# The first attention batch loaded without accumulating transfers: q and k summed by VectorE, v by remainders in the product, and a scheduler that counts issues, bytes and latency of transfers

## The chip, the cores and the metric

The kernel runs on one core of one Trainium2 chip. The metric is the device time of one execution in microseconds, from launch to end; the kernel before was run three times.

## What is computed

Three stages follow one another: a two-part attention, a gated MLP with an RMS norm ahead of it, and a second MLP with a squared ReLU.

```python
# q, k, v: (4 batches, 8 heads, 576 positions, 64), fp32; factor = 4, Sd = 144
q_d = q.reshape(B, H, Sd, factor, D).mean(axis=3)      # the same for k_d, v_d
out_d = sm_attn(q_d, k_d, v_d)                         # softmax attention over 144 means
out_up = np.repeat(out_d, factor, axis=2)
mask = np.abs(pos[:, None] - pos[None, :]) < factor    # local attention, 7 keys a row
out_local = softmax(where(mask, q @ k.T / 8, -1e9)) @ v
x = (out_up + out_local)                               # -> 2304 tokens x 512
xn = x / rms(x) * rms_g
h = silu(xn @ w_gate) * (xn @ w_val) @ w_out           # 512 -> 1536 -> 512
g = s * relu(h @ w_in) ** 2 + b                        # 512 -> 2048
return g @ w_out2                                      # 2048 -> 512
```

The change touches the means over four positions, q_d, k_d and v_d, of the first batch alone.

## The kernel before

The 2304 tokens are worked on in 8 blocks of 288 columns (TB); a batch of attention fills two blocks. A batch has four units, each a pair of heads on 128 partitions: `unit(b, hp)` with hp from 0 to 3 (line 547). A unit makes the local scores of 9 windows (`local`, line 558), the scores of the means (`sd`, lines 587 to 592, from the tile `qd`), both softmaxes, transposes, the product of the means' weights with v (`pvd`, lines 626 to 631, from the tile `vd`), the local product with v (lines 632 to 639), and writes the sum to X (line 645). Then come the squares for the norm; `norm` (line 661) sums them on TensorE, raises them to a power on GpSimd (line 671), spreads them on TensorE and writes X as two f16 halves (lines 679 to 685). The first matmul of the gated MLP (`moe1_gv`, line 793) needs all four units of the batch, that norm for its 288 columns, and part 0 of the gate and value weights.

The sums over four positions come from transfers. `load_unit` (line 517) loads the first of four remainders of q and k with a plain transfer from SyncE's queue (`qkr`, 128x288 f32) and adds the other three with transfers that GpSimd issues with `accum_op=ADD`; the same holds for v (`vr`, 72x256 f32). Transfers into the same tile follow one another, since each adds to what the one before has left. Unit (0,0) alone has q and k summed by VectorE, from the tile `qkT` that the local scores need anyway (`DVE_Q`, line 57, and line 583).

The weights come as 64-bit numbers: `fetch` (line 698) loads a piece into one of eight, then six, then three staging places with SyncE, and ScalarE (two operations) and VectorE (one) decode it. A staging place is free for the next piece when it is decoded. 32 pieces are the gate and value weights (four parts of eight), the next 12 are w_out. `prep_gv` (line 740) then scales and splits them in two f16 halves.

All of this is recorded as a list of operations with their tiles, and `Plan.schedule` (line 310) sets one static order for each engine and for the queues of SyncE and GpSimd; the engines run that order and wait on semaphores. The order comes from a list scheduler with costs: a transfer of GpSimd counts 1.0 for the issue and 3.5 to landing, one of SyncE keeps its queue busy for its bytes (lines 195 to 203). `STEPS` (line 47) is a list of seeds; each disturbs the priorities by `shaken` (line 92). `emit` (line 335) writes the instructions, and where the plan has a gap on TensorE ahead of the first MLP matmul it puts in filler matmuls (line 1131), whose result nobody reads. Every recorded operation has line 352 in the profile.

Batch 1's units are spread among the MLP products of blocks 0 and 1, whose order is a fixed chain. Their v tiles are the four pieces of `VS` (line 447), which in the kernel before also hold batch 0's v.

Of the kernel before, what the change touches and what calls it, by code (L numbers as in the profile page):

```python
# [2 lines left out]

# [19 lines left out]
NP = H // 2  # L23
# [18 lines left out]
RING0 = 15744  # L42
E23 = float(2 ** 23)
SWITCH = 0.095
REACH = 230.0
EARLY = 0.0
STEPS = (
# [5 lines left out]
)  # L53
TOGETHER = 30.0
PE_SUM = ()
PE_SQ = (0,)
DVE_Q = ((0, 0),)
DVE_MASK = (2, 3)
JS = (range(5), range(5, 9))
SIZE = {F32: 4, I32: 4, F16: 2, BF16: 2, U16: 2}  # L60
# [24 lines left out]
def cols(ap):  # L85
    n = 1
    for d in list(ap.ap)[1:]:
        n *= d[1]
    return n


def shaken(key, at, seed):

    r = random.Random(seed)
    key = list(key)
    if r.random() < 0.5:
        mid, width, size, share = r.uniform(0, REACH), r.choice((3, 10, 30)), r.choice((0.5, 2, 8)), r.choice((0.1, 0.5, 1))
        for k, t in enumerate(at):
            if abs(t - mid) < width and r.random() < share:
                key[k] += r.gauss(0, size)  # L100
    else:
        a, n, size = r.randrange(1000), r.choice((2, 5, 15, 40, 100)), r.choice((1, 4, 15))
        by, every = r.gauss(0, size), r.choice((1, 1, 2, 4))
        for k in range(a, a + n * every, every):
            key[k] += by
    return key


class Op:
    __slots__ = ("alts", "fn", "pred", "chain", "early", "tag")  # L110


class Plan:
# [36 lines left out]
    def put(self, alts, fn, reads, writes, chain=False):  # L150
        op = Op()
        op.alts, op.fn, op.chain, op.early = alts, fn, chain, self.early
        op.pred = self.touch(len(self.ops), reads, writes)
        self.ops.append(op)

    def record(self, engs, name, args, kw):
        if self.AP is None:
            self.AP = type(args[0] if args else kw["out"])
        aps = {k: v for k, v in kw.items() if isinstance(v, self.AP)}
        pos = [a for a in args if isinstance(a, self.AP)]  # L160
        outs = [aps.pop(k) for k in ("out", "accum_out") if k in aps]
        if pos:
            outs.append(pos.pop(0))
        ins = pos + list(aps.values())
        reads = [x for a in ins if a.space is not None and "DRAM" not in str(a.space) for x in span(a)]
        writes = [x for a in outs if "DRAM" not in str(a.space) for x in span(a)]
        if engs[0] == "PE":
            t, full = self.pe_time(name, kw)
            single = self.group is None
            if single:  # L170
                self.group = [[], [], [], 0.0, []]
            g = self.group
            g[0].append((name, args, kw))
            g[1].extend(reads)
            g[2].extend(writes)
            if g[4] and g[4][-1] != full:
                t += SWITCH
            g[3] += t
            g[4].append(full)
            if single:  # L180
                self.close()
            return
        big = [a for a in ins if cols(a) > 8 and a.space != PSUM]
        n = max(cols(a) for a in outs + ins)
        scal = sum(cols(a) == 1 for a in ins)
        alts = []
        for e in engs:
            if e == "DVE":
                occ = 0.065 + 1.042e-3 * n + (0.06 if scal else 0)
                alts.append((e, occ, occ + 0.15, len(big) > 1 and n > 32))  # L190
            elif e == "ACT":
                psum = any(a.space == PSUM for a in ins)
                occ = 0.06 + (0.85e-3 if psum else 0.95e-3) * n + 0.1 * scal + (0.09 if "accum_out" in kw else 0)
                alts.append((e, occ, occ + 0.17, False))
            elif e == "POOL" and name == "dma_start":
                alts.append((e, 1.0, 3.5, False))
            elif e == "POOL":
                occ = (0.9 if kw.get("op") == ALU.pow else 0.2) if n < 32 else 0.08 + 2.1e-3 * n * (0.9 if n > 500 else 1)
                alts.append((e, occ, occ + 0.15, n >= 32))
            else:  # L200
                kb = cols(outs[0] if "DRAM" not in str(outs[0].space) else ins[0]) * 4 * 128 / 1e3
                occ = max(0.43, kb / 390)
                alts.append((e, occ, occ + 2.0, False))
        self.put(alts, [(name, args, kw)], reads, writes)

    def pe_time(self, name, kw):
        n = cols(kw["out"])
# [31 lines left out]
    def run(self, pred, succ, chain, key, back):  # L239
# [2 lines left out]
        left = [len(p) for p in pred]  # L242
        ready = [0.0] * n
        engs = ("PE", "ACT", "DVE", "POOL", "SP")
        free = dict(zip(engs, (0.0, 2.5, 0.0, 8.0, 0.7) if not back else (0.0,) * 5))
        wait = {e: [] for e in engs}
        done = [False] * n
        start, where = [0.0] * n, [None] * n
        port, kind = 0.0, None
        at = 0  # L250
        order = []

# [7 lines left out]
        while len(order) < n:  # L260
# [34 lines left out]
            if self.ops[k].chain:  # L295
                at += 1
            order.append(k)
            for j in succ[k]:
                if back:
                    b = self.ops[j].alts[0]  # L300
                    r = t + a[1] + (0.0 if b[0] == "PE" == a[0] else b[2] - b[1])
                else:
                    r = t + (a[1] if e == "PE" == self.ops[j].alts[0][0] else a[2])
                ready[j] = max(ready[j], r)
                left[j] -= 1
                if not left[j]:
                    offer(j)
# [56 lines left out]
def kernel(  # L364
    ctx: ExitStack,
    tc: tile.TileContext,
    qk: bass.AP,
    vwin: bass.AP,
    qkr: bass.AP,
    vr: bass.AP,  # L370
    w_gate: bass.AP,
# [72 lines left out]
    CL = [carve(4 * ZW) for _ in range(2)]  # L444
    DE = [carve(432) for _ in range(2)]
    QD = [carve(288) for _ in range(2)]
    VS = [carve(256) for _ in range(4)]
    vd0, qd0 = VS, [Xf[:, kc, S + 1152:S + 1440] for kc in range(KC)]
    OD = [carve(192) for _ in range(2)]
    TMP = [carve(TB) for _ in range(2)]  # L450
    SQ = carve(S)
    for t, n in [(t, 5) for t in CH] + [(t, 4) for t in CL]:
        nc.gpsimd.memset(t.rearrange("p (j k) -> p j k", j=n)[:, :, WIN:], 1e-9)
    sq0 = [(Xf[:, kc, NT - TB:], W1[:, CO0 + kc * TB:CO0 + kc * TB + TB]) for kc in range(KC)]
    SM = [carve(6) for _ in range(12)]
    turn_ = {}

# [58 lines left out]

    def load_unit(b, hp, st, vd, qd):
        sp.dma_start(out=st["qkT"], in_=qk[b, hp])
        if (b, hp) not in DVE_Q:
            sp.dma_start(out=qd, in_=qkr[b, hp, 0])  # L520
            for i in range(1, 4):
                pool.dma_start(out=qd, in_=qkr[b, hp, i], accum_op=ADD)
        sp.dma_start(out=st["vw"][:WIN], in_=vwin[b, hp])
        sp.dma_start(out=vd, in_=vr[b, hp, 0])
        for i in range(1, 4):
            pool.dma_start(out=vd, in_=vr[b, hp, i], accum_op=ADD)

    def softmax_l(sl, js, b, full):
        m = len(js)
# [17 lines left out]
    def unit(b, hp):  # L547
# [31 lines left out]

        a0 = take("ch", CH).rearrange("p (j k) -> p j k", j=5)  # L580
        a1 = take("cl", CL).rearrange("p (j k) -> p j k", j=4)
        if (b, hp) in DVE_Q:
            dve.tensor_reduce(out=qd, in_=qkT.rearrange("p (a r) -> p a r", r=4), axis=AX.X, op=ADD)
        with plan.pe_group() if b else nullcontext():
            sl = local(JS[0])
# [20 lines left out]
        for g, (a, js) in enumerate(((a0, JS[0]), (a1, JS[1]))):  # L606
# [12 lines left out]
            if n:  # L619
                act.activation(out=PlT[:WIN, js[0] + 4:js[-1] + 1, :], in_=td[:WIN, :n], func=AF.Copy)  # L620
            act.activation(out=PdT[:72, 3 * g:3 * g + 3, :], in_=td[:72, n:n + 3], func=AF.Copy)
        vs = [vd[:, 64 * a:64 * a + 64] for a in range(4)]
        va, vb = (take("mm0", MM[:3]) if b == 0 else take("xv", XV) for _ in range(2))
        pvd, pl = va[:, 320:], (va, vb)
        with plan.pe_group() if b else nullcontext():
            with plan.pe_group():
                for g in range(2):
                    for h in range(2):
                        pe.matmul(out=pvd[64 * h:64 * h + 64].rearrange("p (s q) -> p s q", s=3), lhsT=vs[2 * h + g],
                                  rhs=PdT[:72, g::2, 64 * h:64 * h + 64], start=g == 0, stop=g == 1,  # L630
                                  skip_group_check=True)
            for js, acc in zip(JS, pl):
                with plan.pe_group():
                    for j in js:
                        o = 64 * (j - js[0])
                        for h in range(2):
                            ph = slice(64 * h, 64 * h + 64)
                            pe.matmul(out=acc[ph, o:o + 64], lhsT=vw[:, h, j, :], rhs=PlT[:WIN, j, ph], start=True,
                                      stop=True, skip_group_check=True)
# [535 lines left out]
```

## Time and profile before

| what | us |
|---|---|
| median of 3 runs | 957.06 |
| lowest and highest | 954.49, 960.63 |
| the profiled execution | 962.88 |
| its span, first to last instruction | 960.8 |
| TensorE busy in it | 919.4 |

TensorE is busy for 96% of the span. The profile's page cuts the span in 40 slices and prints for each the busy tenths of every engine, the granted TensorE clock, and the busy share and rate of the 16 DMA engines. The views used below are that page, tables by stretch of time, instructions in order of time, groups of instructions, and the chain of waits that ended last.

### The profile page before, as it was taken

The page shows a single profiled execution, that of the slowest core. Times are in us where ns is not written, and L with a number is a line of the kernel's source. Part 1 is how long each engine was busy: PE and PEld are TensorE (multiplying, and loading weights), DVE is VectorE, ACT ScalarE, POOL GpSimd, SP SyncE. Part 2 cuts the span into 40 slices and gives each one's busy share as a digit, 9 for nine tenths or more (in the row PEclk, how much of TensorE's full clock was granted, in tenths as well). Part 3 has the DMA queues.
Part 4 walks back from the last instruction along what each step waited for, and adds up shares of the span by engine and source line. Part 5 has one row for each costly group of instructions (what it writes and reads, how often), then busy time and mean ns, then how long its engine had stood idle before and what let it go on. Part 6 is the DMA issues. An engine that isn't in the chain of part 4 may idle for free.

```text
span 960.8 us, 26518 instructions
## 1 busy us (share of the span) xinstructions
PE 919.4 (96%) x11191; PEld 807.5 (84%) x11191; DVE 673.4 (70%) x1753; ACT 594.5 (62%) x1494; POOL 94.7 (10%) x128
## 2 busy tenths in 40 slices
PE   5589889999999999999999999999999999999998
PEld 3368678878887888778877878899999999999998
DVE  6366789933675678942825978796969678696875
ACT  6466776723453567733624857695957769595774
POOL 4334322301232100000000000000000000000000
PEclk9777999999999999999999999999999999999999
DMA  9988884302452415400001421000000000000000
GB/s 301 229 243 210 230 236 112 50 2 50 94 120 50 99 46 177 152 1 1 1 1 37 130 76 45 2 2 27 5 24 9 20 27 3 27 7 22 8 21 26
DMA packets 38822, 70.24 MB, mean 73 GB/s; under 512 B 5328, under 2 KB 25808, under 8 KB 38704
## 3 DMA queue, kind: packets, MB, share of 16 engines
q1 hardware_dynamic: 27616, 58.37, 19.5%
q0 software_dynamic: 11088, 10.18, 7.7%
q8 instruction: 87, 1.43, 0.6%
q14 instruction: 31, 0.25, 0.1%
HBM read 63.82 MB, written 4.72 MB: 71 GB/s over the span
## 4 chain that ended last, share of the span: by engine, by line
PE 79%; DMA 9%; DVE 7%; issue 2%; ACT 1%; POOL 1%; ACTq 0%; SPq 0%; POOLq 0%; DVEq 0%
PE bank L352 79%; DMA X<-in_qkr_dram 3%; DMA AREA<-in_vr_dram 2%; DMA R<-in_moe_w_out_dram 2%; DVE AREA L352 2%; DVE W L352 2%; DMA R<-in_moe_w_in_dram 2%; DVE u L352 1%; DVE X L352 1%; ACT AREA L352 1%; POOL AREA L352 1%; DVE n L352 0%; DVE R L352 0%; ACT R L352 0%; POOL X L352 0%
## 5 line engine op out<-in xcount | busy, mean ns | idle before, releaser
L352 PEld LDWEIGHTS <-W 128*128 128x128 f16 (+1 forms) x5728 | 477.2, 98 | 95.0 <-issue 10.6
L352 PE MATMUL bank<-X,W 128*128 128x288 f16 x2304 | 294.2, 287 | 6.5 <-DVE u L352 3.6
L352 PEld LDWEIGHTS <-AREA 128*128 128x128 f16 (+1 forms) x2752 | 172.3, 98 | 0.2
L352 PE MATMUL bank<-W,AREA 128*128 128x144 f16 x2688 | 169.9, 226 | 0.0
L352 PE MATMUL bank<-W 128*128 128x144 f16 (+1 forms) x2176 | 147.7, 226 | 0.2 <-DVE u L352 0.2
L352 PE MATMUL bank<-R,W 128*128 128x288 f16 x1152 | 144.5, 286 | 0.0
L352 DVE SCALAR_TENSOR_TENSOR u<-u,bank 128x288 f32<-128x288 f32 x192 | 86.2, 449 | 52.0 <-PE bank L352 50.2
L352 ACT ACTIVATE R<-R 128x288 f32<-128x288 f32 (+3 forms) x226 | 102.9, 492 | 0.8 <-PE bank L352 0.8
L352 DVE TENSOR_TENSOR R<-bank,R 128x288 f32<-128x288 f32 x128 | 58.0, 454 | 56.8 <-PE bank L352 41.9
L352 ACT ACTIVATE R<-u 128x288 f16<-128x288 f32 x96 | 42.3, 440 | 72.0 <-DVE u L352 71.7
L352 ACT ACTIVATE X<-bank 128x288 f32<-128x288 f32 (+2 forms) x93 | 34.8, 407 | 68.1 <-PE bank L352 67.9
L352 DVE SCALAR_TENSOR_TENSOR W<-R,gsc,W 128x288 f16<-128x288 f32 x136 | 68.9, 510 | 1.3 <-ACT W L352 1.3
L352 PE MATMUL bank<-AREA 64*64 64x70 f32 (+4 forms) x1328 | 64.4, 250 | 4.8 <-DMA AREA<-in_vr_dram 3.5
L352 ACT ACTIVATE W<-R,gsc 128x288 f16<-128x288 f32 x136 | 68.9, 525 | 0.0
L352 PEld LDWEIGHTS bank<-AREA 64*64 64x64 f32 (+2 forms) x1264 | 53.7, 146 | 11.7 <-issue 7.5
L352 DVE TENSOR_TENSOR R<-u,R 128x288 f16<-128x288 f32 x96 | 43.5, 454 | 23.0 <-ACT R L352 22.9
L352 ACT ACTIVATE u<-bank,tsc 128x288 f32<-128x288 f32 x96 | 47.5, 495 | 15.9 <-PE bank L352 14.5
L352 PE MATMUL bank<-R 128*128 128x144 f16 (+3 forms) x760 | 55.1, 225 | 0.2 <-ACT R L352 0.2
L352 POOL DMA_DIRECT2D AREA<-in_vr_dram x48 | 43.2, 918 | 109.4 <-DMA AREA<-in_vr_dram 87.9
L352 DVE TENSOR_TENSOR AREA<-AREA 128x280 f32<-128x280 f32 (+4 forms) x98 | 50.3, 527 | 1.2 <-ACT AREA L352 1.1
L352 PEld LDWEIGHTS <-R 128*128 128x128 f16 (+1 forms) x720 | 45.9, 98 | 0.0
L352 ACT ACTIVATE AREA<-bank 70x512 f32<-70x512 f32 (+3 forms) x86 | 34.9, 452 | 17.5 <-PE bank L352 17.4
(166 smaller groups left out, 1035.6 us busy)
## 6 DMA issues: line engine op xcount, KB each, us to landing
R<-in_moe_w_out_dram SPq DMA_DIRECT2D x28, 512.0 KB
R<-in_moe_w_in_dram SPq DMA_DIRECT2D x16, 512.0 KB
AREA<-in_qk_dram SPq DMA_DIRECT2D x14, 576.0 KB
AREA<-in_qkr_dram POOLq DMA_DIRECT2D x36, 144.0 KB, 3.5
R<-in_moe_w_val_dram SPq DMA_DIRECT2D x13, 384.0 KB
AREA<-in_vwin_dram SPq DMA_DIRECT2D x14, 315.0 KB
W<-in_moe_w_gate_dram SPq DMA_DIRECT2D x11, 384.0 KB
AREA<-in_vr_dram POOLq DMA_DIRECT2D x48, 72.0 KB, 3.8
```

The lines of the kernel that those rows point to most:

```text
L352: getattr(self.real[e], name)(*args, **kw)
```

## The change

For batch 0 the accumulating transfers are gone. q and k of all four units are summed by VectorE from `qkT` (a reduction of 128x1152 to 128x288, until now in unit (0,0) alone). v comes as one transfer of a unit, 72 x 1024 f32 with the four remainders side by side (`vgrp`, laid out on the host), and the product with the weights of the means is made with each remainder apart: 16 matmuls accumulate what 4 did. The tiles of batch 0's v move (two to W1, one to what the four VS pieces were, one to X), and so do the squares for its norm. Batches 1 to 3 keep their accumulating transfers.

The scheduler's costs of transfers change: an issue counts 0.45 on SyncE and 0.95 on GpSimd, the bytes go through one shared resource at 390 or 200 KB a microsecond, and landing adds 2.1. Seeds are drawn by another generator, and there are 63 of them where there were 43.

```diff
-DVE_Q = ((0, 0),)
+DVE_Q, PE_V = (0,), (0,)
...
 STEPS = (
-    537958267, 1059950399, 476105495, 647352053, 680852926, 668825184, 889955854, 76591015, 969828932, 433121505,
...
+    1387849437, 577823238, 1520135813, 1861112737, 965237639, 355233615, 998648951, 809353853, 74572715, 1506962617,
...
-            elif e == "POOL" and name == "dma_start":
-                alts.append((e, 1.0, 3.5, False))
+            elif name == "dma_start":
+                to = outs[0] if "DRAM" not in str(outs[0].space) else ins[0]
+                kb = cols(to) * 4 * to.ap[0][1] / 1e3
+                move = kb / (200 if e == "POOL" else 390)
+                occ = 0.95 if e == "POOL" else 0.45
+                alts.append((e, occ, occ + move + 2.1, False))
...
-                kb = cols(outs[0] if "DRAM" not in str(outs[0].space) else ins[0]) * 4 * 128 / 1e3
-                occ = max(0.43, kb / 390)
-                alts.append((e, occ, occ + 2.0, False))
...
-        free = dict(zip(engs, (0.0, 2.5, 0.0, 8.0, 0.7) if not back else (0.0,) * 5))
+        free = dict(zip(engs, (0.0, 2.5, 0.0, 6.8, 0.7) if not back else (0.0,) * 5))
...
+            late = 0.0
+            if self.ops[k].move and not back:
+                late = max(0.0, moved - t - a[1])
+                moved = max(moved, t + a[1]) + self.ops[k].move
...
-                    r = t + (a[1] if e == "PE" == self.ops[j].alts[0][0] else a[2])
+                    r = t + (a[1] if e == "PE" == self.ops[j].alts[0][0] else a[2] + late)
...
-    VS = [carve(256) for _ in range(4)]
-    vd0, qd0 = VS, [Xf[:, kc, S + 1152:S + 1440] for kc in range(KC)]
+    vs_ = carve(1024)
+    VS = [vs_[:, 256 * i:256 * i + 256] for i in range(4)]
+    qd0 = [Xf[:, kc, S + 1152:S + 1440] for kc in range(KC)]
+    vd0 = [t.rearrange("p (a x) -> p a x", a=4) for t in (W1[:, CO0:CO0 + 1024], W1[:, CO0 + 1024:CO0 + 2048], vs_)]
+    vd0.append(Xf[:, :, S + 1440:S + 1696])
...
-    sq0 = [(Xf[:, kc, NT - TB:], W1[:, CO0 + kc * TB:CO0 + kc * TB + TB]) for kc in range(KC)]
+    sq0 = list(zip(qd0, (X2[:, :TB], X2[:, TB:], W1[:, RING0 + 3072:RING0 + 3360], W1[:, RING0 + 3360:RING0 + 3648])))
...
-        if (b, hp) not in DVE_Q:
+        if b not in DVE_Q:
             sp.dma_start(out=qd, in_=qkr[b, hp, 0])
             for i in range(1, 4):
                 pool.dma_start(out=qd, in_=qkr[b, hp, i], accum_op=ADD)
         sp.dma_start(out=st["vw"][:WIN], in_=vwin[b, hp])
-        sp.dma_start(out=vd, in_=vr[b, hp, 0])
-        for i in range(1, 4):
-            pool.dma_start(out=vd, in_=vr[b, hp, i], accum_op=ADD)
+        if b in PE_V:
+            sp.dma_start(out=vd, in_=vgrp[b, hp].rearrange("p (a x) -> p a x", a=4))
+        else:
+            sp.dma_start(out=vd, in_=vr[b, hp, 0])
+            for i in range(1, 4):
+                pool.dma_start(out=vd, in_=vr[b, hp, i], accum_op=ADD)
...
-        if (b, hp) in DVE_Q:
+        if b in DVE_Q:
             dve.tensor_reduce(out=qd, in_=qkT.rearrange("p (a r) -> p a r", r=4), axis=AX.X, op=ADD)
...
+        w = 4 if b in PE_V else 1
...
                 for g in range(2):
-                    for h in range(2):
-                        pe.matmul(out=pvd[64 * h:64 * h + 64].rearrange("p (s q) -> p s q", s=3), lhsT=vs[2 * h + g],
-                                  rhs=PdT[:72, g::2, 64 * h:64 * h + 64], start=g == 0, stop=g == 1,
-                                  skip_group_check=True)
+                    for i in range(w):
+                        for h in range(2):
+                            pe.matmul(out=pvd[64 * h:64 * h + 64].rearrange("p (s q) -> p s q", s=3),
+                                      lhsT=v4[:, 2 * h + g, i], rhs=PdT[:72, g::2, 64 * h:64 * h + 64],
+                                      start=g == i == 0, stop=g == 1 and i == w - 1, skip_group_check=True)
```

How the order moves is shown at three places.

GpSimd's queue from the first accumulating transfers to the power of the norm of batch 0 (TENSOR_TENSOR with mhalf); X is here the q and k sums of batch 0 (tile qd), AREA the v sums and, with qkr, the sums of batch 1. Before, from the fifth transfer on:

```order
L352 DMA X<-in_qkr_dram 128x288 x3
L352 DMA AREA<-in_vr_dram 72x256 x2
L352 DMA X<-in_qkr_dram 128x288
L352 DMA AREA<-in_vr_dram 72x256 x2
L352 DMA X<-in_qkr_dram 128x288
L352 DMA AREA<-in_vr_dram 72x256 x6
L352 DMA AREA<-in_qkr_dram 128x288
L352 DMA AREA<-in_vr_dram 72x256
L352 DMA AREA<-in_qkr_dram 128x288 x2
L352 DMA AREA<-in_vr_dram 72x256
L352 DMA AREA<-in_qkr_dram 128x288
L352 TENSOR_TENSOR AREA<-AREA,mhalf 96x3
```

In the changed kernel the whole queue from the start to the power, and what follows it, all of it batch 1's but the two powers:

```order
masks.py:199 AFFINE_SELECT ident_b<-ident_b 128x128
L370 DMA AREA<-in_qkr_dram 128x288 x6
L370 DMA AREA<-in_vr_dram 72x256 x4
L370 TENSOR_TENSOR AREA<-AREA,mhalf 96x3 x2
L370 DMA AREA<-in_vr_dram 72x256 x6
L370 DMA AREA<-in_qkr_dram 128x288
```

The 21 transfers of batch 0 are gone from it; ten of batch 1 stand ahead of the power, four of them of v.

SyncE's queue at the start, first before and then changed; qk, vwin and vgrp are the tiles of batch 0's units (AREA, X, R, AREA for unit 0 to 3), the rest weights:

```order
L352 DMA R<-in_moe_w_val_dram 128x768
L352 DMA X<-in_qkr_dram 128x288 x2
L352 DMA AREA<-in_qk_dram 128x1152
L352 DMA R<-in_moe_w_gate_dram 128x768
L352 DMA R<-in_moe_w_val_dram 128x768 x3
L352 DMA rms_sb<-in_moe_rms_g_dram 128x4x1
L352 DMA W_84<-in_moe_w_gate_dram 128x768 x2
L352 DMA AREA<-in_vr_dram 72x256
L352 DMA W_84<-in_moe_w_gate_dram 128x768
L352 DMA X<-in_qk_dram 128x1152
L352 DMA R<-in_moe_w_val_dram 128x768
```

```order
L370 DMA AREA<-in_qk_dram 128x1152
L370 DMA R<-in_moe_w_val_dram 128x768 x2
L370 DMA X<-in_qk_dram 128x1152
L370 DMA R<-in_moe_w_val_dram 128x768
L370 DMA R<-in_moe_w_gate_dram 128x768
L370 DMA rms_sb<-in_moe_rms_g_dram 128x4x1
L370 DMA R<-in_qk_dram 128x1152
L370 DMA AREA<-in_vwin_dram 70x1152
L370 DMA W_84<-in_moe_w_gate_dram 128x768
L370 DMA R<-in_moe_w_val_dram 128x768
L370 DMA X<-in_vwin_dram 70x1152
```

The attention's tiles move ahead of the weights: the second unit's qk was the twelfth transfer on the queue and is now the fourth.

SyncE's queue where batch 1's v begins to be loaded. Before, its loads are spread singly among weights (here the first two of batch 1, after the last of batch 0):

```order
L352 DMA AREA<-in_vr_dram 72x256
L352 DMA R<-in_moe_w_val_dram 128x768
L352 DMA AREA<-in_qkr_dram 128x288
L352 DMA R<-in_moe_w_val_dram 128x768 x2
L352 DMA AREA<-in_vwin_dram 70x1152
L352 DMA W_84<-in_moe_w_gate_dram 128x768
L352 DMA R<-in_moe_w_gate_dram 128x768
L352 DMA W_84<-in_moe_w_gate_dram 128x768
L352 DMA AREA<-in_qk_dram 128x1152
L352 DMA AREA<-in_vr_dram 72x256
```

```order
L370 DMA W_84<-in_moe_w_val_dram 128x768
L370 DMA AREA<-in_qk_dram 128x1152
L370 DMA W_84<-in_moe_w_gate_dram 128x768 x2
L370 DMA AREA<-in_vr_dram 72x256
L370 DMA R<-in_moe_w_val_dram 128x768
L370 DMA AREA<-in_vr_dram 72x256 x3
L370 DMA R<-in_moe_w_gate_dram 128x768
```

Now all four v loads of batch 1 stand together, behind weight pieces that wait for staging places.

## Rows read from the trace of the kernel before

**Rows 1.** The page's busy tenths and granted clock of TensorE in 40 slices.

```profile
PE   5589889999999999999999999999999999999998
...
PEclk9777999999999999999999999999999999999999
```

**Rows 2.** Busy time by stretch: start:end, length, engines, clock, DMA share, GB/s.

```profile
core 0: us, PE busy (x) PEld busy (x) DVE busy (x) ACT busy (x) POOL busy (x), PEclk, DMA share, GB/s
10.00:20.00 10.00, 8.75 (x73) 5.00 (x70) 8.53 (x26) 8.73 (x24) 2.67 (x3) 1.00 1.02 315
50.00:60.00 10.00, 9.27 (x148) 7.74 (x146) 8.90 (x27) 8.01 (x24) 3.80 (x5) 0.95 0.67 152
0.00:69.00 69.00, 42.04 (x492) 31.18 (x493) 38.23 (x108) 39.44 (x105) 26.89 (x56) 0.84 0.94 260
69.00:87.00 18.00, 17.66 (x124) 14.80 (x125) 7.62 (x22) 9.77 (x27) 8.22 (x9) 0.55 0.80 190
87.00:140.00 53.00, 45.21 (x480) 36.00 (x478) 42.83 (x115) 40.96 (x96) 16.52 (x19) 0.97 0.88 230
140.00:175.00 35.00, 34.79 (x408) 28.97 (x406) 34.50 (x103) 24.28 (x64) 8.71 (x10) 1.00 0.53 125
...
260.00:960.80 700.80, 694.86 (x8847) 627.27 (x8845) 505.20 (x1291) 443.44 (x1112) 21.59 (x23) 1.00 0.15 41
```

**Rows 3.** The chain that ended last, from the start to 92 us: start, us, what.

```profile
7.34 8.81 DMA X<-in_qkr_dram
...
23.76 10.21 DMA X<-in_qkr_dram
...
39.44 7.62 DMA AREA<-in_vr_dram
...
57.95 7.44 DMA AREA<-in_vr_dram
...
91.95 5.83 DMA R<-in_moe_w_out_dram
```

**Rows 4.** Single instructions in time: TensorE's last v product and first MLP matmuls, VectorE, GpSimd.

```profile
65.53 3.47 PE L352 MATMUL bank<-AREA 72*64 72x192 f32 x44 [3.51 <-DMA AREA<-in_vr_dram]
...
86.78 4.57 PE L352 MATMUL bank<-X,W 128*128 128x288 f16 x36
...
68.54 0.92 DVE L352 TENSOR_TENSOR X<-bank,AREA 128x320 f32<-128x320 f32 x2 [4.32 <-ACT AREA L352]
...
74.36 1.15 POOL L352 TENSOR_TENSOR AREA<-AREA,mhalf 96x3 f32<-96x3 f32 x1 [3.86 <-DVE AREA L352]
```

**Rows 5.** The page's DMA queues (q1 SyncE's, q0 GpSimd's): packets, MB, share of 16 engines' span.

```profile
q1 hardware_dynamic: 27616, 58.37, 19.5%
q0 software_dynamic: 11088, 10.18, 7.7%
```

**Rows 6.** GpSimd's issues from 6 to 66 us by group: busy, mean ns, idle before.

```profile
L352 POOL DMA_DIRECT2D AREA<-in_vr_dram x12 | 11.0, 966 | 16.4 <-DMA AREA<-in_vr_dram 13.4 <-issue 3.0
L352 POOL DMA_DIRECT2D X<-in_qkr_dram x9 | 8.2, 981 | 16.3 <-DMA X<-in_qkr_dram 16.3
```

**Rows 7.** VectorE's groups from 0 to 70 us: the one q and k sum.

```profile
L352 DVE TENSOR_REDUCE X<-AREA 128x288 f32<-128x1152 f32 x1 | 1.4, 1353 | 2.0 <-DMA AREA<-in_qk_dram 2.0
```

**Rows 8.** TensorE's groups: a unit's v product at 53 us and the last one at 65 us.

```profile
L352 PE MATMUL bank<-X,AREA 72*64 72x192 f32 x8 | 0.9, 339 | 0.0
...
L352 PE MATMUL bank<-AREA 72*64 72x192 f32 x8 | 1.5, 537 | 3.5 <-DMA AREA<-in_vr_dram 3.5
```

**Rows 9.** Tile X up to 70 us: time of its transfers from issue to landing.

```profile
DMA to landing us min/median/max: 4.1/7.9/10.2
```

**Rows 10.** SyncE's issues from 43 to 56 us.

```profile
44.40 0.42 SPq L352 DMA_DIRECT2D AREA<-in_vwin_dram  x1
54.91 0.33 SPq L352 DMA_DIRECT2D W<-in_moe_w_val_dram  x1
```

**Rows 11.** The filler matmuls alone (line 1131) from 0 to 87 us.

```profile
0.00:87.00 87.00, 10.47 (x29) 2.91 (x29) 0.78 0.91 245
```

More of the change, by code (lines that the diff above doesn't have):

```diff
@@ L1 @@
-import random
 from contextlib import ExitStack, contextmanager, nullcontext
@@ L44 @@
 SWITCH = 0.095
-REACH = 230.0
+REACH, FIRST = 230.0, 1200
 EARLY = 0.0
 STEPS = (
[5 rows of a table removed]
[7 rows of a table added]
 )
@@ L92, in shaken, with u @@
 def shaken(key, at, seed):
[L94 to L97, printed above, removed]
+    key, n, x = list(key), len(key), seed
+    def u():
+        nonlocal x
+        x = (x * 1664525 + 1013904223) % 2 ** 32
+        return x / 2 ** 32
+    for _ in range(3):
+        u()
+    if u() < 0.5:
+        mid = u() * REACH
+        width, size, share = (3, 10, 30)[int(u() * 3)], (0.5, 2, 8)[int(u() * 3)], (0.1, 0.5, 1)[int(u() * 3)]
         for k, t in enumerate(at):
-            if abs(t - mid) < width and r.random() < share:
-                key[k] += r.gauss(0, size)
-    else:
-        a, n, size = r.randrange(1000), r.choice((2, 5, 15, 40, 100)), r.choice((1, 4, 15))
-        by, every = r.gauss(0, size), r.choice((1, 1, 2, 4))
-        for k in range(a, a + n * every, every):
+            if abs(t - mid) < width and u() < share:
+                a, b, c = u(), u(), u()
+                key[k] += size * 2 * (a + b + c - 1.5)
+    else:
+        first = int(u() * FIRST)
+        m, every, size = (2, 5, 15, 40, 100)[int(u() * 5)], (1, 1, 2, 4)[int(u() * 4)], (1, 4, 15)[int(u() * 3)]
+        a, b, c = u(), u(), u()
+        by = size * 2 * (a + b + c - 1.5)
+        for k in range(first, min(first + m * every, n), every):
             key[k] += by
@@ L109 @@
 class Op:
-    __slots__ = ("alts", "fn", "pred", "chain", "early", "tag")
+    __slots__ = ("alts", "fn", "pred", "chain", "early", "tag", "move")
 class Plan:
@@ L152, in put @@
         op.alts, op.fn, op.chain, op.early = alts, fn, chain, self.early
+        op.move = 0.0
         op.pred = self.touch(len(self.ops), reads, writes)
@@ L185, in record @@
         scal = sum(cols(a) == 1 for a in ins)
-        alts = []
+        alts, move = [], 0.0
         for e in engs:
@@ L199, in record @@
                 alts.append((e, occ, occ + 0.15, n >= 32))
-            else:
-                kb = cols(outs[0] if "DRAM" not in str(outs[0].space) else ins[0]) * 4 * 128 / 1e3
-                occ = max(0.43, kb / 390)
-                alts.append((e, occ, occ + 2.0, False))
         self.put(alts, [(name, args, kw)], reads, writes)
+        self.ops[-1].move = move
     def pe_time(self, name, kw):
@@ L248, in run @@
         start, where = [0.0] * n, [None] * n
-        port, kind = 0.0, None
+        port, moved, kind = 0.0, 0.0, None
         at = 0
@@ L368 @@
     vwin: bass.AP,
+    vgrp: bass.AP,
     qkr: bass.AP,
@@ L621, in unit @@
             act.activation(out=PdT[:72, 3 * g:3 * g + 3, :], in_=td[:72, n:n + 3], func=AF.Copy)
-        vs = [vd[:, 64 * a:64 * a + 64] for a in range(4)]
+        w = 4 if b in PE_V else 1
+        v4 = vd.rearrange("p a (r d) -> p a r d", r=w) if b in PE_V else vd.rearrange("p (a r d) -> p a r d", a=4, r=w)
         va, vb = (take("mm0", MM[:3]) if b == 0 else take("xv", XV) for _ in range(2))
@@ L1158 @@
     groups = v.reshape(B, NP, 2, 2, 72, 4, D)
+    laid["vgrp"] = groups.transpose(0, 1, 4, 2, 3, 5, 6).reshape(B, NP, 72, 16 * D)
     laid["qkr"] = laid["qk"].reshape(B, NP, 128, 2 * SD, 4).transpose(0, 1, 4, 2, 3)
     laid["vr"] = groups.transpose(0, 1, 5, 4, 2, 3, 6).reshape(B, NP, 4, 72, 4 * D)
-    for name in ["qk", "vwin", "qkr", "vr"] + _INS:
+    for name in ["qk", "vwin", "vgrp", "qkr", "vr"] + _INS:
         a = _np.ascontiguousarray(laid[name])
```

10 rows, old and new, of the table STEPS are left out of this document.

## The prediction

> **What bounds the kernel now.** Start with the page's slices [rows 1]: TensorE is at nine tenths from the seventh slice on (24 us each), and only the first slices show gaps and a granted clock below full. The table by stretch says how much is there [rows 2]. After 140 us TensorE is idle for 0.2 us of 35, and for 5.9 us of the last 700.8: it is the bound, and the change adds or takes nothing there. Up to 87 us it is idle for 27.3 us (69.0 less 42.0 and 18.0 less 17.7), and its mean granted clock is 0.84 up to 69 us and 0.55 from there to 87: a mixture of its two levels, 1.2 and 2.4 GHz. Between 87 and 140 us 7.8 us are idle. So at most some 35 us of idle time, with the slow clock and 10.5 us of fillers [rows 11], are to be had, all ahead of 140 us.
>
> What ends the waits there is the third view, the chain of waits [rows 3]. Three accumulating transfers of q and k (the first and the last 8.8 and 10.2 us) and, later, transfers of v (7.6 and 7.4 us) stand on it, one behind the other. The last v lands at 65.4 us, and TensorE, idle for 3.5 us, begins the last v product at 65.53; VectorE writes the last of X from 68.54 to 69.46, and the first MLP matmul follows at 86.78 [rows 4]. From 92 us on the chain stands on w_out pieces [rows 3].
>
> **What the change takes away.** Batch 0 has 9 accumulating transfers of q and k (0.147 MB each) and 12 of v (0.074 MB): 2.21 MB. The queues' rates [rows 5]: q1 moves 58.37 MB in 19.5% of 960.8 us, which is 187.4 us, so 311 GB/s; q0 moves 10.18 MB in 74.0 us, 138 GB/s. Accumulated bytes thus hold the 16 DMA engines 2.3 times as long. 2.21 MB at 138 GB/s are 16.0 us; the seven plain loads that go with them (3 of 0.147 and 4 of 0.074 MB) are 2.4 us; the four new vgrp loads (0.295 MB each) cost 3.8 us. Net 14.6 us of DMA time. GpSimd also loses 21 issues of 0.97 us, and the 29.7 us in which it waited for one accumulation to land before the next [rows 6].
>
> **What it adds.** VectorE sums q and k of three more units: 3 x 1.353 = 4.1 us [rows 7]. TensorE gets 12 more matmuls a unit, 48 in all. The trace records each fp32 matmul as two, and two run beside one another in the two halves of the array; 4 matmuls keep it busy for 0.9 us at full clock and 1.5 us at the lower one [rows 8]. So 48 cost at most 12 x 0.9 = 10.8 us, or 18 us at the lower clock; less the tail of each group, which is paid once, I take 8.5.
>
> **The start, step by step.** What is late next when the sums no longer come by transfer? VectorE had done 38.2 us of work by 69 us [rows 2]. With the three sums it is 42.3. In the stretches where it was fed, at 10 to 20 and 50 to 60 us, it was busy for 8.5 and 8.9 of 10 [rows 2]; at 0.87 it needs 48.6 us. The first qk is now first in SyncE's queue, so I let it begin at 5 to 6 us. That writes the last of X at about 54.5 instead of 69.5: 15 us earlier. Are other things ready? TensorE had 42.0 us of work by 69 us; with 8.5 it is 50.5, just under 54.5, so the added products are hidden, but only if they run at the higher clock; at the lower one 60 us stand against 54.5 and 5 to 6 us of the gain go. ScalarE had 39.4 and gets nothing. The transfers of batch 0 are now 12 plain ones of 4.8 MB in all, and with about 10 weight pieces of 0.39 MB ahead of them 8.7 MB, 28 us at 311 GB/s: no longer late. From the last of X to the first MLP matmul were 17.3 us, most of it TensorE at a mean clock of 0.55 [rows 2, 4]; I keep it and lose 1 us for the power (below). First MLP matmul at about 73: **14 us earlier**.
>
> **Does the gain last?** Between 87 and 140 us the DMA engines are busy for 0.88 of the time, and the chain stands on weights. Up to 140 us they were busy for 0.94 x 69 + 0.80 x 18 + 0.88 x 53 = 125.9 us. Without 14.6 of these it is 111.3, and at the same mean share of 0.90 it takes 123.7 us instead of 140: the weights can come 16 us earlier, which covers the 14. The 7.8 us of idle time between 87 and 140 I leave as they are: the scheduler now knows that transfers share the engines, and may place the decodes better (bound -7.8), or the static order may meet a late piece elsewhere (bound about the longest such wait on the chain, one w_out piece of 5.8 us [rows 3]); I take 0. VectorE is full from 140 to 175 us (34.5 of 35) while TensorE has no gap, so a shift of both costs nothing; I charge 1 us for the added work there.
>
> Sum for the profiled execution: 962.9 - 14 + 1 = 949.9. It lies 5.8 us over the median of the runs, 957.06; the same 13 us off the median give **944**. About 1% is what a measurement of this kernel can tell from no change.
>
> **A rule that speaks against it.** The rows show accumulations of 144 KB in the first 70 us landing 4.1 to 10.2 us after their issue, median 7.9 [rows 9]. The Trainium skill (DMA: Bandwidth & Descriptors, Anatomy of one DMA, SWDGE path) gives a transfer issued by GpSimd about 2.0 us and its bytes at 436 GB/s: an estimate of 2.3 us for 144 KB, with no charge for the addition. By it the chain of three would be a third as long, and little would be won beyond the bytes. The trace disagrees: 7.9 us stand against 2.3.
>
> **Rivals.**
>
> *Only bytes count.* If an accumulation is slow only because it waits behind weights on busy engines, removing it frees its bytes and no more: 2.21 + 0.74 - 1.18 = 1.77 MB, at 311 GB/s 5.7 us. Then the first MLP matmul comes early, but the weights of parts 1 to 3 hold the chain, and idle time moves to 75 to 130 us. For it: the DMA share of 0.94 up to 69 us. Against it: the rate of q0 is taken over the whole span, where the engines are mostly free. Time 957 - 5.7 = 951.
>
> *The better order pays too.* If the new costs also take away the idle time between 87 and 140, and most fillers, the gain is 13 + 7.8 + about 4 = 25: 932. For it: those waits are decodes behind late transfers, which the old costs left out. Against it: the static order still knows no landing time exactly.
>
> *Slower: the power behind batch 1's v.* GpSimd now has four v accumulations of batch 1 ahead of the norm's power, and SyncE's loads for them stand behind weight pieces that wait for staging places. VS holds unit (0,2)'s v, so they cannot go earlier than its product. SyncE has stood for 10.1 us at such a place [rows 10]. If it does so here, then the wait, four issues of 0.97 and a landing of 4.1 come to some 18 us behind the last of X, where before the power ran 4.9 us after it [rows 4, 9]. That takes 13 of the 14 us; with the products at the lower clock (another 5 to 6) the kernel is 4 us slower: 961. It decides from a power later than about 19 us after the last of X. Against it: the loads need only unit (0,2), with a whole unit still to come.
>
> **How the numbers follow.** Forecast, 6 to 20 us faster: 0.62. Only bytes, 0 to 6 faster: 0.18. Better order, over 20: 0.11. Slower than before: 0.09, of which over 1%: 0.05. The 1% line is at 947.5; of the forecast's band about nine tenths lie below it, so faster is 0.56 + 0.11 = 0.67, slower 0.05, the rest 0.28. The range goes from the better order (932, a little under) to no change: 931 to 957.
>
> **What would show it.** In the changed profile: no accumulating transfer ahead of 20 us on the chain; the last write of X near 55 and the first MLP matmul near 73; VectorE above eight tenths in the first 50 us; TensorE gapless from about 125 us; q0's bytes down to 8.0 MB and its share below 6.2%. Wrong would be a first MLP matmul after 82, a gap on a weight piece that takes back over 8 us before 140, or a power that waits on GpSimd's queue.

## The result, and the profile after

The changed kernel takes 946.81 us (median of 4 runs, 945.02 to 948.00) beside 958.48 for the kernel before on the same chip: a ratio of 0.9881, interval 0.9841 to 0.9922. On a second chip it was 0.9813 [0.9775, 0.9851]. The forecast was 944 in a range of 931 to 957, with a gain of over 1% the likeliest outcome. The time is 3 us off it. The median lies 1.2% below the kernel before; this interval alone (0.8 to 1.6%) does not exclude a gain under 1%, that of the second chip (1.5 to 2.2%) does. The steps that led there were not those that were forecast. The profiled execution took 948.0 us with a span of 946.2 (forecast 949.9, before 962.88).

The same table by stretch as [rows 2], of the changed kernel:

```profile
core 0: us, PE busy (x) PEld busy (x) DVE busy (x) ACT busy (x) POOL busy (x), PEclk, DMA share, GB/s
0.00:69.00 69.00, 53.18 (x624) 42.59 (x629) 44.73 (x117) 44.49 (x117) 15.27 (x41) 0.87 0.98 272
69.00:87.00 18.00, 17.70 (x164) 15.44 (x167) 14.14 (x37) 14.17 (x37) 9.65 (x11) 0.82 0.96 247
87.00:140.00 53.00, 51.64 (x593) 42.63 (x591) 50.58 (x140) 43.88 (x102) 8.72 (x10) 1.00 0.70 195
140.00:175.00 35.00, 35.00 (x396) 29.15 (x394) 33.50 (x88) 24.35 (x62) 7.92 (x9) 1.00 0.45 90
175.00:260.00 85.00, 83.62 (x853) 67.62 (x853) 40.15 (x117) 32.58 (x92) 17.32 (x19) 0.98 0.30 59
```

Read the first row against the third of [rows 2]. TensorE did 53.2 us of work instead of 42.0 and VectorE 44.7 instead of 38.2, but the DMA engines went from 0.94 busy to 0.98. They were relieved of transfers and filled up with others. In the third row TensorE's idle time fell from 7.8 us to 1.4, and in the last 1.4 us are idle.

The single instructions that answer to [rows 4], and the first v product, in the changed kernel (in brackets, the idle time just before and what ended it):

```profile
28.98 5.39 PE L370 MATMUL bank<-AREA,W 72*64 72x192 f32 x32 [3.66 <-DMA W<-in_vgrp_dram]
63.03 0.82 DVE L370 TENSOR_TENSOR X<-bank,AREA 128x320 f32<-128x320 f32 x2
66.75 1.78 POOL L370 TENSOR_TENSOR AREA<-AREA,mhalf 96x3 f32<-96x3 f32 x1
77.27 7.51 PE L370 MATMUL bank<-X,W 128*128 128x288 f16 x60
184.00 19.67 PE L370 MATMUL bank<-R,W 128*128 128x288 f16 x156
```

The last of X is written at 63.85 us instead of 69.46 and the first MLP matmul begins at 77.27 instead of 86.78: 9.5 us earlier. The last row is the first product with R, a mark further on; in the kernel before the same row reads:

```profile
200.07 19.27 PE L352 MATMUL bank<-R,W 128*128 128x288 f16 x156
```

Here 16.1 us are won. So the start gave 9.5, and the idle time that is gone between 87 and 140 us gave 6.4 more. Of these 1.5 were lost again by the end of the span (14.6 less than before), 1.3 of them between 175 and 260 us, where TensorE waits for a power on GpSimd. One profile does not fix these marks closely: in a second one of the same kernel, on another chip, the last of X is written at 61.60 us, the first MLP matmul begins at 75.13, and 2.5 us are idle between 87 and 140.

The chain of waits from the start, in place of [rows 3] (start, us, what):

```profile
4.28 10.09 DMA R<-in_qk_dram
14.39 14.46 DMA W<-in_vgrp_dram
28.98 11.25 PE bank L370 x104
...
43.48 10.01 DMA R<-in_moe_w_gate_dram
...
59.60 1.79 ACT W L370 x4
...
64.31 2.17 PE bank L370 x18
66.72 4.00 PE bank L370 x24
```

No accumulating transfer stands on it. Three plain loads do, each of them 10 to 14 us long for 288 to 576 KB, and from 53 us on ScalarE, VectorE and TensorE in turn. The queues, in place of [rows 5], and GpSimd's first accumulations up to 66 us, in place of [rows 6]:

```profile
q1 hardware_dynamic: 27400, 58.82, 20.5%
q0 software_dynamic: 8640, 7.97, 6.2%
```

```profile
L370 POOL DMA_DIRECT2D AREA<-in_qkr_dram x6 | 5.4, 906 | 48.5 <-DMA AREA<-in_qkr_dram 48.5
```

The page prints the shares to 0.1%, which is 1 us here, so the comparison is made with the packets' own times in the trace, over 16 engines. q0's fell from 74.2 us to 58.2, by 16.0 as forecast. But q1's rose from 187.2 to 194.0, by 6.8 where 1.4 was forecast (to 191.4 in the second profile). The engines' time fell by 9.2 us, not by 14.6. GpSimd, which now has only batch 1 ahead, waits for it.

### The profile page after: what moved, and what is told of

It reads as the page before. It is cut to its first block, busy times and chain, and to the rows that moved or that the text cites. A ratio compares the mean times of both kernels' runs of the same rounds, so it can differ in the third digit from the quotient of the medians.

```text
span 946.2 us, 26664 instructions
## 1 busy us (share of the span) xinstructions
PE 920.6 (97%) x11276; PEld 811.8 (86%) x11283; DVE 678.2 (72%) x1756; ACT 595.2 (63%) x1494; POOL 76.3 (8%) x107
## 4 chain that ended last, share of the span: by engine, by line
PE 85%; DMA 6%; DVE 4%; ACT 2%; issue 1%; POOL 0%; SPq 0%; POOLq 0%; ACTq 0%; DVEq 0%
PE bank L370 85%; DMA W<-in_vgrp_dram 2%; DMA R<-in_moe_w_in_dram 1%; DMA R<-in_qk_dram 1%; DMA R<-in_moe_w_gate_dram 1%; DVE W L370 1%; DVE AREA L370 1%; DVE X L370 1%; ACT AREA L370 1%; DMA R<-in_moe_w_out_dram 1%; DMA W<-in_moe_w_val_dram 1%; ACT W L370 1%; DVE u L370 0%; POOL AREA L370 0%; DVE R L370 0%
## 5 line engine op out<-in xcount | busy, mean ns | idle before, releaser
L370 PE MATMUL bank<-X,W 128*128 128x288 f16 (+1 forms) x2336 | 297.6, 287 | 0.0
L370 ACT ACTIVATE R<-u 128x288 f16<-128x288 f32 x96 | 42.3, 440 | 69.3 <-DVE u L370 69.1
L370 PE MATMUL bank<-AREA 64*64 64x70 f32 (+4 forms) x1312 | 61.0, 244 | 0.8 <-ACT AREA L370 0.8
L370 ACT ACTIVATE u<-bank,tsc 128x288 f32<-128x288 f32 x96 | 47.5, 495 | 18.9 <-PE bank L370 17.3
L370 PEld LDWEIGHTS bank<-AREA 64*64 64x64 f32 (+2 forms) x1248 | 51.1, 142 | 7.3 <-issue 4.1
L370 PE MATMUL bank<-ident_f,AREA 128*70 128x128 f32 (+2 forms) x288 | 40.3, 280 | 6.9 <-POOL AREA L370 3.3
```

The lines of the kernel that those rows point to most:

```text
L370: getattr(self.real[e], name)(*args, **kw)
```

## The experiments

Three groups ran on three chips, each beside the kernel before (961.5 to 962.1 us there). The theory was that of the prediction; the rivals were that only bytes count, and that the new order, not the missing transfers, brings the time.

### Data and costs apart

Four kernels without the seeds (`STEPS = ()`), so that the order is the scheduler's own: the kernel before; batch 0's new sums with the old costs; the old sums with the new costs; both.

```diff
-STEPS = (
...
+STEPS = ()
```

> The kernel before with the list of seeds left empty, so the scheduler's own best order of four rounds stands. It is the base of a table of four: old or new way of making the sums, old or new costs of transfers, all without seeds. If the seeds only polish the order, it is 0 to 10 us slower than the kernel before (957 to 968). If the seeds carry the order, 10 to 30 us slower.

> Batch 0 without accumulating transfers, old costs of transfers, no seeds. Theory A (the removed sums make the start earlier, the new costs take away the waits between 87 and 140 us, about 9 and 6 us): 8 to 12 us faster than e1, first MLP matmul some 10 us earlier, idle time of TensorE between first MLP matmul and full load still 5 us or more. Theory B (the gain is the order's, from the new costs and seeds): within 3 us of e1.

> Sums by accumulating transfers as before, new costs of transfers, no seeds. Theory A: 3 to 8 us faster than e1, with the start nearly as late as in e1 and fewer waits behind it. Theory B: 10 us or more faster than e1, with an earlier first MLP matmul too. A third possibility: slower, because the new costs see the accumulations as the bound and put long gaps and fillers on TensorE.

> The changed kernel with the list of seeds left empty. Theory A: within 5 us of the changed kernel (947 to 952), since sums and costs make the gain. Theory B, with the seeds carrying it: 955 or more.

| kernel | us | ratio to before | first MLP matmul | first R product | idle 87 to 140 |
|---|---|---|---|---|---|
| before, no seeds | 962.35 | 1.0012 [0.9996, 1.0027] | 87.78 | 198.44 | 4.9 |
| new sums only | 954.35 | 0.9932 [0.9908, 0.9956] | 77.43 | 188.24 | 6.4 |
| new costs only | 969.53 | 1.0077 [1.0048, 1.0107] | 100.23 | 206.76 | 3.7 |
| both | 954.38 | 0.9910 [0.9878, 0.9943] | 84.76 | 191.05 | 2.7 |

Without seeds the sums alone give 8 us. The costs alone lose 7, where the theory had 3 to 8 us of gain; the third possibility came. In that kernel TensorE stands from 29.3 to 63.3 us before one accumulation of q and k, first on fillers, then idle. The rows are from its instructions in time and from its waits of TensorE up to 140 us (in total, times, longest):

```profile
29.32 17.23 PE L1131 MATMUL bank<-mask,ones_b 128*128 128x512 bf16 x79
...
PE bank L352 <- DMA X<-in_qkr_dram: 16.7, 1, 16.7
```

The kernel before without seeds has such a wait too (14.0 us), but up to 87 us only 10.6 us of fillers where this one has 24.3.

With both, the time is that of the sums alone, but it is made up otherwise: the first MLP matmul comes 7.3 us later and 3.7 us less are idle after it. In these profiles, one of each kernel, the new costs trade the start for the stretch behind it. What stands in that stretch under the old costs is VectorE (TensorE's waits from 87 to 140 us, new sums only):

```profile
PE bank L357 <- DVE AREA L357: 2.5, 1, 2.5
PE bank L357 <- DVE u L357: 1.9, 2, 1.8
PE bank L357 <- DVE m L357: 1.4, 1, 1.4
```

The seeds were worth nothing to the kernel before (0.3% at most). To the changed kernel they are worth something: without them it takes 954.38 us, more than the 947 to 952 of the theory. With its own 63 seeds the first MLP matmul comes at 77.27 and 75.13 on two chips instead of 84.76; in time that is 3 to 9 us (ratios of 0.9881 and 0.9813 against 0.9910), taken across chips and so no closer.

### The transfers alone

The kernel before with its order unchanged on every engine; at emission batch 0's accumulating transfers are skipped, all 21 or only the 9 of q and k.

```diff
             for name, args, kw in o.fn:
+                if "accum_op" in kw and any(kw["in_"] is x for x in self.marked):
+                    continue
```

> The kernel before in its own order, word for word on every engine and on SyncE's queue; only the 21 accumulating transfers of batch 0 are not issued, so batch 0's sums hold one remainder of four. No work is added. Theory (the DMA engines, full up to 87 us, are the bound of the start, and 2.21 MB at 138 GB/s hold them 16 us): first MLP matmul 72 to 76 us instead of 86.8, time 9 to 14 us less than before (ratio 0.985 to 0.991). Rival, only bytes count (2.21 MB at 303 to 311 GB/s, 7 us): first MLP matmul near 80, at most 7 us less (0.993 or above). Rival, the gain of the start is lost at the weights because the old order is kept: first MLP matmul near 75, but idle time of 10 us or more between there and 140, and 2 to 5 us less.

> As the kernel without batch 0's 21 accumulating transfers, but only the 9 of q and k are not issued (1.33 MB); the 12 of v (0.88 MB) stay. Theory (engines' time): 0.6 of what all 21 give, at the first MLP matmul too, so 5 to 8 us less than before. Rival (the chains of three transfers behind one another are the bound, and v's chain comes last): the first MLP matmul moves by less than 3 us, since the last v transfer before landed at 65.4 us, and the time by less than 3.

Without all 21: 946.87 us, ratio 0.9851 [0.9816, 0.9886], 15.3 us less (11 to 18 by the interval). This is above what the theory gave (9 to 14) and twice what the bytes alone could (7). Single instructions of this kernel, and its table by stretch:

```profile
52.91 0.91 DVE L355 TENSOR_TENSOR X<-bank,AREA 128x320 f32<-128x320 f32 x2 [1.53 <-ACT AREA L355]
70.43 4.57 PE L355 MATMUL bank<-X,W 128*128 128x288 f16 x36
183.93 19.27 PE L355 MATMUL bank<-R,W 128*128 128x288 f16 x156
```

```profile
0.00:69.00 69.00, 52.16 (x598) 41.76 (x605) 43.97 (x124) 47.14 (x125) 14.36 (x40) 0.85 0.93 271
69.00:87.00 18.00, 16.62 (x171) 13.26 (x172) 16.09 (x43) 15.62 (x41) 9.49 (x11) 1.00 0.91 219
87.00:140.00 53.00, 45.80 (x510) 37.39 (x508) 44.86 (x118) 37.60 (x89) 12.10 (x14) 0.97 0.78 212
```

The last of X comes at 53.82, the first MLP matmul 16.4 us earlier than before, and all of it is still there at the R product (16.1 earlier). The 7.2 us idle between 87 and 140 are those of before: with the old order they stay.

Without q and k's nine: 955.53, ratio 0.9926 [0.9902, 0.9951], 6.6 us less, the first MLP matmul at 80.12, 6.7 earlier. That is 0.43 of what all 21 give, where 9 of 21 are 0.43 by number and 1.33 of 2.21 MB are 0.60 by bytes. The 5 to 8 of the theory holds, its share of 0.6 does not, and the rival (under 3) falls. The chain of this kernel shows what is left:

```profile
24.11 8.22 DMA AREA<-in_vr_dram
32.67 8.47 DMA AREA<-in_vr_dram
41.48 5.99 DMA AREA<-in_vr_dram
47.81 0.58 POOL AREA L355
48.39 3.62 DMA AREA<-in_vr_dram
52.36 7.00 DMA AREA<-in_vr_dram
```

With q and k gone, the v accumulations, one behind the other, hold the chain from 24 to 59 us. That the gain follows the number of transfers (0.43) rather than their bytes (0.60) fits a start bound by landings one after another. It does not prove it: with these two intervals (4.7 to 9.4 us of 11 to 18) a share of 0.60 is just possible, and the 15.3 us of all 21 are also near the 16.0 of engine time.

### The order of the changed kernel, one cost at a time

The changed kernel again, and three variants in its own order: 12 of a unit's 16 v products of batch 0 left out; the vgrp loads some places earlier in SyncE's queue; and batch 0's q and k sums made twice.

```diff
+                if any(kw.get("lhsT") is x for x in self.marked):
+                    continue
...
+        for k, before in zip(groups, (4, 6, 7, 9)):
+            order.remove(k)
+            order.insert(order.index(weights[before]), k)
...
+                if any(kw.get("out") is x for x in self.marked) and name == "tensor_reduce":
+                    getattr(self.real[e], name)(*args, **kw)
```

> The changed kernel once more, on the chip of e6, e7 and e8, as their base: ratio to the kernel before 0.988, as the first measurement had it (0.984 to 0.992).

> The order of the changed kernel word for word, but 12 of the 16 products of v in each unit of batch 0 are left out, so only the first remainder is counted. It prices the added products where they stand. My prediction's theory (hidden beside VectorE and transfers): 0 to 2 us faster than the changed kernel. Rival (they stand on the path, at the lower clock in the first unit, 5.4 us for 16): 5 to 9 us faster.

> The order of the changed kernel, but the four loads of batch 0's v stand 1 to 6 places earlier in SyncE's queue, each ahead of weight pieces. In the changed kernel the first v is on the chain for 14.5 us and TensorE waits 3.7 us for it. Theory A (the start waits for that load): first v product at about 25 instead of 29 us, first MLP matmul 2 to 4 us earlier, the whole 2 to 4 us faster. Rival (the DMA engines are full from 10 to 70 us, so the weight pieces behind come later by as much): the first v product earlier, but within 1 us of the changed kernel in all.

> The order of the changed kernel with each of the four sums of q and k of batch 0 made twice on VectorE, 4 x 1.35 = 5.4 us more. If VectorE's sums are hidden: 0 to 1.5 us slower than the changed kernel. If VectorE is the bound of the start, as my prediction had it: 4 to 5.4 us slower.

| kernel | us | ratio to before | first MLP matmul |
|---|---|---|---|
| changed, again | 944.68 | 0.9813 [0.9775, 0.9851] | 75.13 |
| a quarter of the v products | 943.64 | 0.9794 [0.9756, 0.9832] | 73.90 |
| vgrp earlier | 944.12 | 0.9813 [0.9770, 0.9857] | 73.64 |
| sums twice | 945.80 | 0.9820 [0.9781, 0.9858] | 74.53 |

All four are within one another's intervals, and the first of them, the changed kernel on this chip, was better than its expectation (0.984 to 0.992). Its two profiles differ by 2.1 us at the first MLP matmul, so the differences of 0.6 to 1.5 us in the last column show nothing by themselves. Leaving out 48 products gives 1.0 us: they are hidden. Twice the sums add 5.5 us to VectorE's work up to 69 us (50.37 against 44.85), the first MLP matmul does not come later and the time grows by 1.1 us, which is within the intervals: VectorE had room. With vgrp earlier TensorE's wait for it (3.4 us in the changed kernel on this chip) is gone, and another stands at the same product, which begins at 28.21 us instead of 25.26, not earlier as expected:

```profile
28.21 5.39 PE L381 MATMUL bank<-AREA,W 72*64 72x192 f32 x32 [4.51 <-ACT AREA L381]
```

### Batch 1

Two kernels: in the changed kernel's order, batch 1's 24 accumulating transfers skipped (as above, for batch 1); and the changed kernel with batch 1's q and k summed by VectorE too, its order made anew.

```diff
-DVE_Q, PE_V = (0,), (0,)
+DVE_Q, PE_V = (0, 1), (0,)
```

> The changed kernel in its own order; batch 1's 24 accumulating transfers (2.65 MB, 19 us of the engines at 136 GB/s), which in the changed kernel run between 38 and 77 us, are not issued, so batch 1's sums hold one remainder of four. Theory (the engines are the bound of the changed kernel's start too): the last of X and the first MLP matmul come 3 to 8 us earlier than in the changed kernel (69 to 74 instead of 75 to 77), time 3 to 7 us less than the changed kernel. Rival (past 40 us TensorE, VectorE and ScalarE in turn are the bound): first MLP matmul and time within 1.5 us of the changed kernel.

> The changed kernel with batch 1's q and k summed by VectorE as well: 12 accumulating transfers (1.77 MB) and 4 plain loads less, 5.4 us more of VectorE, and an order that the scheduler makes anew. Theory (engines' time): 2 to 5 us less than the changed kernel if VectorE has room. Rival (VectorE, busy 50.6 of 53 us between 87 and 140, is the bound there, and the disturbed priorities were made for the other list of operations): 3 to 8 us more than the changed kernel, with waits of TensorE on VectorE between 87 and 140 us.

Without batch 1's transfers: 942.69 us, ratio 0.9817 [0.9770, 0.9863], which does not part from the changed kernel's two ratios. In the trace the DMA share from 69 to 87 us falls from 0.96 to 0.58, and the first MLP matmul comes at 73.61, 1.5 or 3.7 us earlier than in the two profiles of the changed kernel. That mark lies in the theory's 69 to 74; in time, against the first ratio 6 us are gained, against the second none. So 19 us of engine time, mostly past 40 us, bring a few us at most, and between theory and rival this run does not decide.

With batch 1's sums on VectorE: 951.80, ratio 0.9903 [0.9866, 0.9940], above both ratios of the changed kernel, though its interval meets that of the first. The rival's place for the loss, VectorE between 87 and 140 us, is wrong (TensorE is idle for 1.6 us there). The first MLP matmul comes at 80.01, 2.7 or 4.9 us later than in the two profiles of the changed kernel, and between 140 and 175 us 2.4 us are idle where it had none. So most of the loss is ahead of that matmul, where this is TensorE's largest wait (up to 140 us: in total, times, longest):

```profile
PE bank L370 <- ACT X L370: 7.7, 2, 6.2
```

The seeds were drawn for another list of operations; whether others would bring the 2 to 5 us of the theory was not tried. No version with the whole computation beat the changed kernel by more than its interval.

## Why the prediction was right, and where it was not

*The accumulating transfers hold the start.* Right, and more than forecast: the removal alone, with the order kept, gives 15.3 us. The reason given was engine time (2.21 MB at 138 GB/s, 16.0 us). The run without q and k's nine suggests that the length of the chains counts as well; which of the two it is stays open. The changed kernel is not the removal alone. Without seeds its sums give 8 us, and the 63 seeds, for which the sum had no term, bring 3 to 9 more.

*Only bytes count* falls: 5.7 us net were its forecast and 7 its limit, 15.3 were measured.

*"That writes the last of X at about 54.5"; "First MLP matmul at about 73".* Measured 63.85 and 77.27 (61.60 and 75.13 in the second profile). 53.82 and 70.43 were reached by the kernel that drops the transfers and adds nothing. The step that failed is the one that named VectorE as late next (0.87 busy, 48.6 us for 42.3 of work): doubling the sums cost nothing that can be measured, and VectorE was 0.65 busy up to 69 us. On the chain stand plain loads in its place. At the last of X 9.4 of the 15 us were missing (7.1 in the second profile). The term behind it was wrong the other way: from the last of X to the first MLP matmul 17.3 us were kept and 1 added, and 13.4 were measured (13.5 in the second profile).

At the first MLP matmul 4.7 to 6.8 us were lost against the kernel that adds nothing, and no one cost explains them: leaving out products, moving vgrp, doubling the sums or dropping batch 1's transfers each moves it by 0.6 to 3.7 us, hardly more than the 2.1 between two profiles of one kernel. The new costs are not what lost them either: with the old costs and the new sums it comes at 77.43. What is left is the added loads and work together, in an order made anew for them; which part of it stays open.

*"No longer late: 28 us at 311 GB/s".* Wrong for vgrp, which is on the chain from 14.4 to 28.9 us; its last packets moved at 41 us. The estimate took the mean rate of the whole span for full engines, on which plain packets took longer (next paragraph).

*DMA time, 14.6 us net.* q0's part was right (16.0), q1's was mis-sized by 5.4 us. Grouping the trace's packets of the whole span by queue and size shows where (count, mean time of one, their time over 16 engines):

```
                             before                   after
q1 3072 bytes (weights)      4096, 147 ns, 37.5 us    4096, 159 ns, 40.6 us
q1 4096 bytes (vgrp)         none                      216, 303 ns,  4.1 us
q1 1024 bytes (vgrp in X)    none                      288,  74 ns,  1.3 us
q1 1024 bytes (v)            1152,  59 ns,  4.2 us     864,  65 ns,  3.5 us
q1 1152 bytes (q and k)      1920,  66 ns,  7.9 us    1536,  71 ns,  6.8 us
```

Plain packets took longer on the fuller engines. The weights cost 3.1 us more, vgrp 5.4 where 3.8 were taken, and the plain loads that went gave back 1.8 instead of 2.4. By the prediction's own reckoning 9.2 us of engine time bring the weights 10 us earlier and not 16, and yet 16.1 were still there at the first R product. The tables by stretch suggest why: the engines were fuller early, with 84.9 us of work up to 87 us instead of 79.3, and 37.1 instead of 46.6 from there to 140.

*"The 7.8 us of idle time between 87 and 140 I leave as they are; I take 0".* Mis-sized: 6.4 of them went (5.3 in the second profile). By the table of four, the new costs remove part (4.9 to 3.7, 6.4 to 2.7). This was half of the rival *the better order pays too*; its other half, fillers, came as well (18 of 5.4 us up to 87 us instead of 29 of 10.5 [rows 11]), without an earlier start to show for it. So the sum came out by luck, by two errors that cancel: -9.5 instead of -14 at the start, -6.4 instead of 0 behind it.

*Products hidden.* Right: leaving three quarters out gives 1.0 us, within the interval. The first unit's ran at the lower clock (5.39 us at a granted 0.50), the later ones took 2.82 each at 1.00: 13.9 us for the four, 9 to 10 more than before, where 8.5 were taken.

*Slower: the power behind batch 1's v.* It did not happen. The power began 2.9 us after the last of X (66.75 against 63.85), directly behind the three v issues of 64.57 us, and 19 us was the point from which it would decide.

*The rule for a transfer issued by GpSimd.* The rows up to 70 us showed 7.9 us for 144 KB [rows 9], against an estimate of 2.3 worked out from the Trainium skill (DMA: Bandwidth & Descriptors, Anatomy of one DMA). The changed kernel's transfers of the same size show that most of the difference is load. Up to 60 us, at a DMA share of 0.98, and from 300 to 600 us, at 0.20 (lines of issues in these stretches: count, KB each, median us to landing):

```profile
AREA<-in_qkr_dram POOLq DMA_DIRECT2D x6, 144.0 KB, 7.6
...
AREA<-in_qkr_dram POOLq DMA_DIRECT2D x5, 144.0 KB, 3.3
```

At 0.20 3.3 us stand against 2.3, so there the trace contradicts the rule by 1 us, not by 5.6 as the prediction had it. The rest of the 5.6 came with engines that the weights had filled. All of these transfers accumulate, so what a plain one issued by GpSimd takes is not shown.

## What to carry to other kernels

Where transfers must land one after another, look at their landings on the chain of waits and not at their bytes alone: here the bytes gave 7 us at most, and the removal 15.3. Skip the suspected transfers at emission with the order kept: that gives the worth of the removal before a scheduler mixes it with a new order. And new costs in a planner are a change of their own, that has to be run alone: here they lost 7 us by themselves.

## What was not expected of the hardware

In the first 68 us of the kernel before, an accumulating packet of 1152 bytes holds a DMA engine for 117 ns, a plain one of the same size for 57. From 300 to 600 us, at a DMA share of 0.22, it is 138 against 64. So full engines are not what doubles it, though they can cost a plain packet something as well (89 ns in the changed kernel's first 68 us). All the accumulating packets are on GpSimd's queue and the plain ones on SyncE's: whether the addition or the queue costs this was not separated. The landing time goes with the load: 7.6 us on full engines and 3.3 on nearly free ones, in the changed kernel.
